# Landmark attention and a gated MLP on one core: the landmark values are folded into the gate and value weights

## The chip, the cores and the metric

The kernel runs on one core of a Trainium2 chip. Its time is the device time of one execution in microseconds (us). Five engines work side by side, each through its own list of instructions in order: TensorE (PE) multiplies matrices, VectorE (DVE), ScalarE (ACT) and GpSimd (POOL) work element by element, and SyncE (SP) issues the transfers (DMA) between the chip's main memory (HBM) and the on-chip memory (SBUF). PE writes its sums into eight PSUM banks, each 128 partitions by 512 fp32 values.

## The reference

The inputs are q, k and v (8 batches, 8 heads, 576 rows, 64 wide), three weight matrices in fp64 and a gain.

```python
q_lm = q.reshape(B, H, m, S // m, D).mean(axis=3)      # m = 32 landmarks
k_lm = k.reshape(B, H, m, S // m, D).mean(axis=3)
A, Bm, C = sm(q, k_lm), sm(q_lm, k_lm), sm(q_lm, k)    # sm: softmax of a.b^T / 8
Z = Bm^T / (|Bm|_1 |Bm|_inf)
for _ in range(6): Z = 2 * Z - Z @ Bm @ Z
attn = A @ Z @ C @ v
x = attn.transpose(0, 2, 1, 3).reshape(4608, 512)
xn = x / sqrt(mean(x * x) + 1e-6) * rms_g
out = (silu(xn @ w_gate) * (xn @ w_val)) @ w_out       # d_ff = 1536
```

For one batch and head, A is 576x32 and W = Z C v is 32x64. The rows of x for a batch are the eight products A W side by side, 8 x 64 = 512 wide.

## The kernel before, in words

Most products are split for accuracy: an operand is rounded to fp32r (`hi`), the rest is a second operand (`lo`), and a product is the three matmuls hi.hi, hi.lo, lo.hi. Rounding is an ACT copy, the rest a DVE or POOL subtraction.

**Attention.** Eight heads form two groups `g` of four. `stage1` sums q and k over blocks of 18 rows (`lmT`, L341), makes the scores `sC` and `sA` in PSUM, and the softmax of C on rows. Its `back` part does the softmax of A in transposed blocks `tA`, turns it into `AT`, splits that into `AS`, transposes E and makes `pCV` = C v. `newton` iterates with `PV`, which holds Z and Z C v together, and ends with `Whi` and `Wlo`. `second` makes x of a batch (`pO`, copied into `xr`), its mean square (`pss`, `pms`), the reciprocal root, and scales x by it and by the gain (L586). x goes to HBM (`x_dram`) and, split into `xhi` and `xlo` (L612, L614), into chunk tiles.

**MLP, direct part.** `d_ff` is 12 slices of 128. `mlp_chunk` takes 512 tokens through the first four slices: for gate and for value 12 matmuls of 512 columns over a contraction of 512, then silu on ACT (L269), product on DVE (L270), the split of the hidden slice (L273, L274), then output matmuls `pso` by groups of 128 tokens, whose partial sums go to HBM (`p_dram`). There are nine chunks. Seven are interleaved with the attention of later batches; the order is written by `Mixer`, which keeps a clock of assumed matmul times and lets attention parts in when their waits are due. All engines then run in the order so written.

**MLP, Strassen part.** After attention two passes take four slices each, through six units of 768 tokens. Gate and value together are multiplied by a 7-product scheme on halves (`product`, 384 columns, contraction 256, six matmuls each), with sums on DVE and splits of seven operands per unit from reloaded x (`prepare`, L825 and L826). Each pass loads partial sums, adds (L941) and stores. Weights arrive as fp64; `Weights` and `Fast` decode them on ACT and DVE (L725 to L733) tile by tile.

Of the kernel before, what the change touches and what calls it, by code (L numbers as in the profile page):

```python
# [79 lines left out]
def nystrom_moe_kernel(  # L80
# [18 lines left out]
    DFF = w_gate.shape[1] // 2  # L99
    M = 32  # L100
# [13 lines left out]
    mxs = ExitStack()  # L114
    mx_ = mxs.enter_context(tc.tile_pool(name="mx", bufs=2, reuse_waits="tile"))
# [12 lines left out]
    VZ = cst.tile([P, G, 3 * D], F32, name="VZ")  # L128
    nc.gpsimd.memset(VZ, 0.0)
# [15 lines left out]

    class Weights:


        def __init__(self, slots):
            self.slots = dict(slots)  # L150
            self.plan([(f, nm) for f, _ in slots for nm in "gv"] + [(f, "o") for f, _ in slots])
            self.done = {}

        def plan(self, order):
            self.order, self.queue, self.raws = list(order), list(order), {}

        def get(self, f, nm):
            while (f, nm) not in self.done:
                self.load_next()
            return self.done[f, nm]  # L160
# [17 lines left out]
        def load_next(self):  # L178
# [3 lines left out]
            slot = self.slots[f]  # L182
# [4 lines left out]
            wf = mp.tile(shp, F32, name="w32", tag="w32", bufs=WB)  # L187
            w = wf.bitcast(I32)
            nc.scalar.activation(wf, whead.bitcast(F32), AF.Abs)
            nc.vector.tensor_scalar_max(wf, wf, 2.0**-15)  # L190
# [685 lines left out]
    def unit(u, fs, xs, hs, src, last, after):  # L876
# [92 lines left out]
        for _ in nxt:  # L969
            pass  # L970
# [79 lines left out]
```

## Time and profile before

| | |
|---|---|
| timed runs (3) | median 1067.74 us, 1064.79 to 1068.96 |
| span of the profiled execution | 1067.6 us, mean granted PE clock 0.958 |
| PE, PEld (weight loads) busy | 1005.0 us (94%), 838.9 us (79%) |
| DVE, ACT, POOL busy | 738.9 us (69%), 485.2 us (45%), 90.0 us (8%) |
| transfers | 123.82 MB, mean 116 GB/s |
| first and second chunk's first hidden slice | 85.5 us, 160.1 us |

The profile gives the profiled execution's time as its span; it lies 0.1 us under the median of the timed runs, so nothing outside the span has to be added. A row of a group of instructions names line, engine, operation, output and inputs, shapes and count, then busy time, mean ns of one, idle time of the engine before them and what ended it. A row in order of time begins with start and length in us.

### The profile page before, as it was taken

To read this page: it belongs to the slowest core of one execution; us is meant where nothing else is said; L and a number is where in the kernel's file an instruction comes from. 1 tells how busy PE (TensorE), PEld (TensorE's weight loads), DVE (VectorE), ACT (ScalarE), POOL (GpSimd) and SP (SyncE) were. 2 spreads that over 40 slices of the span, in tenths; PEclk is the share of its full clock that TensorE was granted. 3 is DMA by queue.
4 is the path that set the end of the run, shared out by engine and by line. 5 is a ranking of instruction groups with operands and counts; after the bars stand their busy time and mean duration, and the time that the engine had idled before them with its cause. 6 is when DMAs were issued, how large, how long until landed. Compare 5 with 4: busy or idle time off the path is not lost.

```text
span 1067.6 us, 17593 instructions
## 1 busy us (share of the span) xinstructions
PE 1005.0 (94%) x6918; PEld 838.9 (79%) x6918; DVE 738.9 (69%) x1503; ACT 485.2 (45%) x988; POOL 90.0 (8%) x86
## 2 busy tenths in 40 slices
PE   5649989999999999999999999999999999999998
PEld 4326655676767677787989899998989989899997
DVE  7899959848565452787895665847897475675743
ACT  3536554446353533455644352433745344352431
POOL 2243221203020110100000000000000000000000
PEclk7669989999999999999999999999999999999999
DMA  9346443505130110543534505143250422505122
GB/s 336 118 141 204 145 148 96 190 23 196 64 111 34 53 64 21 182 131 97 180 114 151 170 8 178 34 144 130 88 177 20 160 87 91 177 1 177 50 69 79
DMA packets 62946, 123.82 MB, mean 116 GB/s; under 512 B 5520, under 2 KB 27024, under 8 KB 61840
## 3 DMA queue, kind: packets, MB, share of 16 engines
q1 hardware_dynamic: 62864, 122.71, 34.0%
q8 instruction: 54, 0.88, 0.4%
q14 instruction: 28, 0.23, 0.1%
HBM read 84.94 MB, written 37.75 MB: 115 GB/s over the span
## 4 chain that ended last, share of the span: by engine, by line
PE 74%; DVE 17%; DMA 3%; ACT 3%; issue 2%; POOL 1%; SPq 0%; ACTq 0%; DVEq 0%; POOLq 0%
PE pso L141 24%; PE px L141 18%; PE pz L141 9%; PE psg L141 6%; PE psv L141 5%; PE pw L141 4%; PE pO L141 2%; PE pn L141 2%; DVE xr L586 2%; DMA srawv<-in_moe_w_val_dram 1%; DVE lmT L341 1%; DVE h L274 1%; PE pCV L141 1%; DVE xlo L614 1%; DVE s L270 1%
## 5 line engine op out<-in xcount | busy, mean ns | idle before, releaser
L141 PE MATMUL pso<-whio,h 128*128 128x512 f32 x288 | 101.3, 421 | 6.1 <-DVE h L274 3.2
L141 PE MATMUL pso<-solo,h 128*128 128x512 f32 x432 | 100.4, 390 | 0.0
L825 ACT CAST x<-xf 128x768 fp32r<-128x768 f32 x84 | 68.0, 833 | 69.7 <-DVE xf L843 54.2
L141 PEld LDWEIGHTS pso<-solo,h 128*128 128x128 f32 x432 | 81.0, 188 | 16.3
L141 PE MATMUL pso<-sowhio,h 128*128 128x512 f32 x288 | 90.9, 390 | 0.0
L941 DVE TENSOR_TENSOR ob<-ob,pso 128x512 f32<-128x512 f32 x72 | 48.8, 684 | 49.1 <-PE pso L141 48.8
L826 DVE TENSOR_TENSOR x<-xf,x 128x768 fp32r<-128x768 f32 x84 | 79.1, 953 | 5.0 <-ACT x L825 5.0
L873 DVE TENSOR_TENSOR h<-c,h 128x384 fp32r<-128x384 f32 x96 | 53.2, 554 | 37.5 <-ACT h L872 37.5
L141 PE MATMUL psg<-xhi,whig 128*128 128x512 f32 x144 | 61.1, 424 | 16.5 <-ACT xhi L612 16.5
L141 PEld LDWEIGHTS pso<-whio,h 128*128 128x128 f32 x288 | 57.0, 200 | 22.7 <-DVE h L274 5.1
L894 ACT COPY c<-px 128x384 f32<-128x384 f32 x48 | 23.0, 480 | 109.3 <-PE px L141 109.3
L872 ACT CAST h<-c 128x384 fp32r<-128x384 f32 x96 | 49.5, 515 | 34.5 <-DVE c L883 28.2
L141 PE MATMUL psg<-xlo,whig 128*128 128x512 f32 x144 | 60.9, 423 | 2.8 <-DVE xlo L614 2.5
L141 PEld LDWEIGHTS pso<-sowhio,h 128*128 128x128 f32 x288 | 54.1, 188 | 11.0
L141 PE MATMUL pso<-wloo,h 128*128 128x512 f32 x144 | 60.5, 420 | 0.0
L141 PE MATMUL psg<-xhi,wlog 128*128 128x512 f32 x144 | 60.3, 419 | 0.0
L141 PE MATMUL px<-x,swfs1c 128*128 128x384 f32 x288 | 57.8, 334 | 1.3 <-ACT c L901 1.3
L141 PE MATMUL psv<-xhi,whiv 128*128 128x512 f32 x144 | 58.4, 406 | 0.0
L141 PE MATMUL psv<-xlo,whiv 128*128 128x512 f32 x144 | 58.3, 405 | 0.0
L141 PE MATMUL psv<-xhi,wlov 128*128 128x512 f32 x144 | 57.9, 402 | 0.0
L141 PE MATMUL px<-x,swfs2c 128*128 128x384 f32 x288 | 57.8, 335 | 0.0
L141 PE MATMUL px<-x,swfs0c 128*128 128x384 f32 x288 | 57.8, 335 | 0.0
(223 smaller groups left out, 2226.7 us busy)
## 6 DMA issues: line engine op xcount, KB each, us to landing
xd<-xr SPq DMA_DIRECT2D x8, 1152.0 KB, 5.0
pd<-ob SPq DMA_DIRECT2D x36, 256.0 KB, 2.2
xf<-xd SPq DMA_DIRECT2D x8, 1152.0 KB, 7.1
ob<-pd SPq DMA_DIRECT2D x36, 256.0 KB, 3.4
pe<-ob SPq DMA_DIRECT2D x36, 256.0 KB, 2.7
ob<-pe SPq DMA_DIRECT2D x36, 256.0 KB, 3.1
out_dram<-ob SPq DMA_DIRECT2D x36, 256.0 KB, 2.7
vt<-in_v_dram SPq DMA_DIRECT2D x16, 512.0 KB, 4.3
```

The costliest lines, as they stand in the source:

```text
L141: tc.keep_in_program_order(nc.tensor.matmul(*args, **kw))
L270: nc.vector.tensor_mul(s, s, banks[1])
L274: nc.vector.tensor_sub(h2, s, h1.bitcast(F32))
L341: nc.vector.tensor_reduce(lmT[:, z], qk[z].rearrange("p h (m c) -> p h m c", c=LM), axis=AX.X, op=ALU.add)
L586: last = nc.vector.scalar_tensor_tensor(xr[:, kk], xr[:, kk], gsb[:, kk : kk + 1], Rt, op0=ALU.mult, op1=ALU.mult)
L614: eng.tensor_sub(xlo[:, kk, off : off + n], xr[:, kk, pos : pos + n], xhi[:, kk, off : off + n].bitcast(F32),)
L825: nc.scalar.copy(t[:, 0], src)
L826: nc.vector.tensor_sub(t[:, 1], src, t[:, 0].bitcast(F32))
L872: nc.scalar.copy(hi, s)
L873: nc.vector.tensor_sub(lo, s, hi.bitcast(F32))
L894: nc.scalar.copy(c1, px)
L941: nc.vector.tensor_add(ob, ob, bank.pop(t))
```

## The change

x is never made for the MLP. Since x = A W by heads, `xn @ w` = (A/rms) @ (W gain w): `mix_weights` multiplies, for each batch and each pair of slices, the gate and value weights (fp32, 512 columns: gate and value of two slices) by the batch's landmark values `WT` (transposed, with the gain). The result (`pM`, split into `Mhi`, `Mlo`) has 8 x 32 = 256 rows. `second` still makes x once to get its mean square (`pO` is only squared), then scales `tA` by the reciprocal root, transposes, splits it into `an` and stores it to HBM for the second pass. `mlp` then multiplies `Mhi`/`Mlo` by `an`, 2 x 3 matmuls of 288 columns for each of gate and value and each half of a batch's 576 tokens. The Strassen code goes. There are two passes of six slices; the first, interleaved with attention, stores partial sums, the second reloads `an` and the partial sums and adds. A batch holds 4.5 groups of 128 tokens, so odd batches first copy the last 64 columns of each hidden slice on POOL (the `TAIL` copy). The maximum in the weights' decoding moves from DVE to POOL; gate and value weights are no longer split. The pool `pg` has four PSUM banks, before three; after attention nothing takes the other four.

```diff
--- before.py
+++ after.py
...
-            wf = mp.tile(shp, F32, name="w32", tag="w32", bufs=WB)
+            if nm == "o":
+                wf = mp.tile(shp, F32, name="w32", tag="w32", bufs=WB)
+            else:
+                pair = f // 2
+                if pair not in self.gv:
+                    self.gv[pair] = self.place("gv", pair), []
+                at = (f % 2 * 2 + "gv".index(nm)) * P
+                wf = self.gv[pair][0][:, :, at : at + P]
+                self.gv[pair][1].append(nm)
             w = wf.bitcast(I32)
             nc.scalar.activation(wf, whead.bitcast(F32), AF.Abs)
-            nc.vector.tensor_scalar_max(wf, wf, 2.0**-15)
+            nc.gpsimd.tensor_scalar_max(wf, wf, 2.0**-15)
...
-            hi = wp.tile(shp, F32R, name=f"whi{nm}{f}", tag=f"whi{nm}{slot}", bufs=1)
-            lo = wp.tile(shp, F32R, name=f"wlo{nm}{f}", tag=f"wlo{nm}{slot}", bufs=1)
-            nc.scalar.copy(hi, wf)
-            nc.gpsimd.tensor_sub(lo, wf, hi.bitcast(F32))
-            self.done[f, nm] = (hi, lo)
+            if nm == "o":
+                hi, lo = self.place("o", f)
+                nc.scalar.copy(hi, wf)
+                nc.gpsimd.tensor_sub(lo, wf, hi.bitcast(F32))
+                self.out[f] = hi, lo
...
-    def mlp_chunk(i, wts, fs, xhi, xlo, between=lambda: None):
-        nf = len(fs)
-        hh, hl = [], []
-        for fi, f in enumerate(fs):
...
+    def weight_order(f0):
+        fs = range(f0, f0 + NF1)
+        return [(f, nm) for f in fs for nm in "gv"] + [(f, "o") for f in fs]
...
+    def mix_weights(wts, b, pair):
+
+        wgv = wts.get("gv", pair)
+        ps = [pg.tile([P, 4 * P], F32, name="pM", tag="pg") for g in range(G)]
+        for h in range(4):
+            for g in range(G):
+                n = pos(g, h)
+                mm(
+                    ps[g][rows(n), :],
+                    WT[half(h), b, 2 * g + h // 2, rows(n % 2)],
+                    wgv[half(h), 2 * g + h // 2, :],
+                    start=True,
+                    stop=True,
+                )
+        hi = mp.tile([P, G, 4 * P], F32R, name="Mhi", tag="Mhi", bufs=2)
+        lo = mp.tile([P, G, 4 * P], F32R, name="Mlo", tag="Mlo", bufs=2)
+        for g in range(G):
+            nc.scalar.copy(hi[:, g], ps[g])
+            nc.vector.tensor_sub(lo[:, g], ps[g], hi[:, g].bitcast(F32))
+        mixed[b, pair] = hi, lo
+
+    hs = [wp.tile([P, 2, TAIL + S], F32R, name=f"h{f}", tag=f"h{f}") for f in range(NF1)]
+
+    def mlp(wts, b, f0, an, store, part, following):
+        pairs = [f0 // 2 + n for n in range(NPAIR)]
+        if (b, pairs[0]) not in mixed:
+            mix_weights(wts, b, pairs[0])
+            yield 1.1
+        for n, pair in enumerate(pairs):
+            if n + 1 < NPAIR and (b, pairs[n + 1]) not in mixed:
+                mix_weights(wts, b, pairs[n + 1])
+                yield 1.1
+            mhi, mlo = mixed.pop((b, pair))
+            for i in range(2):
+                s = mp.tile([P, S], F32, name="s", tag="s", bufs=2)
+                for e in range(2):
+                    cols = slice(e * HS, (e + 1) * HS)
+                    banks = []
+                    for z in range(2):
+                        ps = pg.tile([P, 512], F32, name=f"ps{'gv'[z]}", tag="pg")
+                        at = slice((2 * i + z) * P, (2 * i + z + 1) * P)
+                        for g in range(G):
+                            for w, a in ((mhi, 0), (mhi, 1), (mlo, 0)):
+                                mm(
+                                    ps[:, :HS],
+                                    w[:, g, at],
+                                    an[:, a, g, cols],
+                                    start=(g == 0 and w is mhi and a == 0),
+                                    stop=(g == G - 1 and w is mlo),
+                                )
+                                yield MMG
+                        banks.append(ps[:, :HS])
+                    nc.scalar.activation(s[:, cols], banks[0], AF.Silu)
+                    nc.vector.tensor_mul(s[:, cols], s[:, cols], banks[1])
+                h = hs[2 * n + i]
+                if b % 2:
+                    nc.gpsimd.tensor_copy(h[:, :, :TAIL], h[:, :, S : S + TAIL])
+                nc.scalar.copy(h[:, 0, TAIL:], s)
+                nc.vector.tensor_sub(h[:, 1, TAIL:], s, h[:, 0, TAIL:].bitcast(F32))
+        t0 = (b * S + P - 1) // P if b % 2 == 0 else b * S // P
+        t1 = (b + 1) * S // P
+        base = b * S - TAIL
+        groups = list(range(t0, t1))
+        obs = {t: part(t) for t in groups[:2]}
+        for at in range(0, len(groups), 2):
+            some = groups[at : at + 2]
+            bank = {t: pg.tile([P, DM], F32, name="pso", tag="pg") for t in some}
+            order = [(t, n) for t in some for n in range(NF1 - 1)] + [(t, NF1 - 1) for t in some]
+            for t, n in order:
+                sl = slice(t * P - base, (t + 1) * P - base)
+                hi, lo = wts.get("o", f0 + n)
+                mm(bank[t], hs[n][:, 0, sl], hi, start=(n == 0), stop=False)
+                yield MMO
+                mm(bank[t], hs[n][:, 0, sl], lo, start=False, stop=False)
+                yield MMO
+                mm(bank[t], hs[n][:, 1, sl], hi, start=False, stop=(n == NF1 - 1))
+                yield MMO
+                if n == NF1 - 1:
+                    store(t, bank[t], obs.pop(t))
+            for t in groups[at + 2 : at + 4]:
+                obs[t] = part(t)
+            if at == 0 and following():
+                mix_weights(wts, b + 1, pairs[0])
+                yield 1.1
...
-            Whi = sm.tile([P, 2, P], F32R, name="Whi", tag="Whi", bufs=1)
-            Wlo = sm.tile([P, 2, P], F32R, name="Wlo", tag="Wlo", bufs=1)
-            pW = pa.tile([P, 2, P], F32, name="pW", tag="pa")
...
+                    r = rows(rho(g, h))
+                    mm(pW[rows(pos(g, h)), g], Bs[r, g, :], VF[r, g, :], start=True, stop=True)
+            W = sm.tile([P, 2, 2, D], F32, name="W", tag="W", bufs=2)
+            nc.vector.tensor_copy(W, pW.unsqueeze(2).broadcast_to([P, 2, 2, D]))
+            nt["W"] = W
+            yield 0.4, WW
+            pT = pa.tile([P, NK, 2 * M], F32, name="pT", tag="pa")
+            for g in range(2):
+                tp(
+                    pT[:, 2 * g : 2 * g + 2].rearrange("p j n -> p (j n)"),
+                    W[:, g].rearrange("p a d -> p (a d)"),
+                    ident,
+                )
+            nc.vector.tensor_mul(WT[:, b], pT, gsb.unsqueeze(2).broadcast_to([P, NK, 2 * M]))
+            yield 0.3, WW
+            stage["wt"] = b
...
-            (Whi, Wlo), ATs = nt["W"], nt["AT"]
-            xr = ap.tile([P, NK, S], F32, name="xr", tag="xr", bufs=2)
...
+                po = [pa.tile([P, HS], F32, name="pO", tag="pa") for n in range(4)]
+                for h in range(4):
+                    for g in range(2):
+                        r = rows(pos(g, h))
+                        mm(po[2 * g + h // 2][half(h)], W[r, g, 0, :], ATs[g][r, cols], start=True, stop=True)
+                sq = ap.tile([P, NK, HS], F32, name="sq", tag="sq", bufs=2)
+                for n in range(4):
+                    nc.scalar.activation(sq[:, n], po[n], AF.Square)
+                sqs.append(sq)
+                yield 0.8, OWL
...
-            for kk in range(NK):
-                last = nc.vector.scalar_tensor_tensor(
-                    xr[:, kk], xr[:, kk], gsb[:, kk : kk + 1], Rt, op0=ALU.mult, op1=ALU.mult
-                )
-            nc.sync.dma_start(x_dram[b], xr)
...
+            an = mp.tile([P, 2, 2, S], F32R, name="an", tag="an", bufs=2)
+            for g in range(2):
+                eng = nc.gpsimd if g else nc.vector
+                eng.tensor_mul(tAs[g], tAs[g], r1.unsqueeze(2).broadcast_to([P, NB, M]))
+            for g in range(2):
+                af = ap.tile([P, S], F32, name="af", tag="af", bufs=1)
+                nc.vector.transpose(af, tAs[g].rearrange("p n m -> p (n m)"))
+                nc.scalar.copy(an[:, 0, g], af)
+                last = nc.vector.tensor_sub(an[:, 1, g], af, an[:, 0, g].bitcast(F32))
+            nc.sync.dma_start(a_dram[b], an.bitcast(F32).rearrange("p a g s -> p (a g s)"))
+            ans[b] = an
...
-    class Fast:
...
-    def product(ps, ws, xs, p, start):
...
-    def unit(u, fs, xs, hs, src, last, after):
...
+        def keep(t, ps, ob):
+            ob = mp.tile([P, DM], F32, name="ob", tag="ob", bufs=2)
+            nc.scalar.copy(ob, ps)
+            nc.sync.dma_start(p_dram[t], ob)
...
+    def load_an(b):
+        an = lp.tile([P, 2, 2, S], F32R, name="anl", tag="anl", bufs=2)
+        nc.sync.dma_start(an.bitcast(F32).rearrange("p a g s -> p (a g s)"), a_dram[b])
+        return an
...
+    def finish(t, ps, ob):
+        nc.vector.tensor_add(ob, ob, ps)
+        nc.sync.dma_start(out[t * P : (t + 1) * P, :], ob)
+
+    late = Weights(weight_order(NF1), place_late)
+    mix.add(late.stream(WAIT1 / 2))
+    mix.fill(mlp(early, B - 1, 0, ans.pop(B - 1), keep, lambda t: None, lambda: False))
+    nxt = load_an(0)
+    for b in range(B):
+        an, nxt = nxt, load_an(b + 1) if b + 1 < B else None
+        mix.fill(mlp(late, b, NF1, an, finish, load_part, lambda b=b: b + 1 < B))
```

How the order of instructions moves. First, PE where the second half of the program begins. Before, one slice of a Strassen unit: `px`, `pz`, `pw` are the products' banks, `x` the seven split operands, `swfs0c` the weights.

```order
L141 MATMUL px<-x_5426,swfs0c_5092 128x384 x6
L141 MATMUL pz<-x_5430,swfs0c_5096 128x384 x6
L141 MATMUL px<-x_5434,swfs0c_5097 128x384 x6
L141 MATMUL pw<-x_5437,swfs0c_5093 128x384 x6
L141 MATMUL pz<-x_5440,swfs0c_5094 128x384 x6
L141 MATMUL px<-x_5444,swfs0c_5098 128x384 x6
L141 MATMUL px<-x_5426,swfs1c_5263 128x384 x6
L141 MATMUL pz<-x_5430,swfs1c_5267 128x384 x6
```

These rows stand no more in the changed program.

Now, where the second pass begins, with two mixes and the first gate/value sections (`anl` is the reloaded attention weights, `lgv` the late weights):

```order
L104 MATMUL pM<-lgv_5927,WT 32x512 x8
L104 MATMUL pM<-lgv_6050,WT 32x512 x8
L104 MATMUL psg<-anl,Mhi 128x288 x2
L104 MATMUL psg<-anl,Mlo 128x288
L104 MATMUL psg<-anl,Mhi 128x288 x2
L104 MATMUL psg<-anl,Mlo 128x288
L104 MATMUL psv<-anl,Mhi 128x288 x2
L104 MATMUL psv<-anl,Mlo 128x288
L104 MATMUL psv<-anl,Mhi 128x288 x2
L104 MATMUL psv<-anl,Mlo 128x288
```

Products of 384 columns in runs of six are replaced by mixes of eight matmuls and sections of six with 288 columns.

Second, DVE in the front of the program, around the first hidden slices. Before, around the first slice's product (L270) and split (L274) of the first chunk; `w_1041` is a weight tile in decoding, `lmT` a landmark sum:

```order
L190 TENSOR_SCALAR w_1041<-w_1041 128x512
L405 TENSOR_REDUCE mA<-tA 128x18
L191 TENSOR_SCALAR w_1041<-w_1041 128x512
L270 TENSOR_TENSOR s<-s,psv 128x512
L489 TENSOR_TENSOR PV<-p_992,nden 128x2x32
L388 TENSOR_TENSOR ss<-ss 128x1
L194 SCALAR_TENSOR_TENSOR w_1041<-wrawv_1039,w_1041 128x512
L389 TENSOR_SCALAR ss<-ss 128x2
L341 TENSOR_REDUCE lmT<-qk_984 128x64
L390 RECIPROCAL rs<-ss 128x2
L274 TENSOR_TENSOR h_1005<-s,h_1005 128x512
```

Of this, the maximum (L190) leaves DVE and the chunk's product and split become those of half and whole batches.

Now, around the second hidden slice of the first batch (L288 product, L293 split):

```order
L288 TENSOR_TENSOR s<-s,psv 128x288
L170 TENSOR_SCALAR wgv_799<-wgv_799 128x4x128
L414 TENSOR_REDUCE mA<-tA 128x18
L293 TENSOR_TENSOR h_130<-s,h_130 128x576
L173 SCALAR_TENSOR_TENSOR wgv_799<-wrawv_1001,wgv_799 128x4x128
L170 TENSOR_SCALAR w_1030<-w_1030 128x512
L176 SCALAR_TENSOR_TENSOR wgv_799<-wrawv_1001,wgv_799 128x4x128
L173 SCALAR_TENSOR_TENSOR w_1030<-wrawo_1028,w_1030 128x512
L418 TENSOR_REDUCE sumA<-tA 128x18
L176 SCALAR_TENSOR_TENSOR w_1030<-wrawo_1028,w_1030 128x512
L419 TENSOR_SCALAR sumA<-sumA 128x18
L347 TENSOR_REDUCE lmT<-qk_989 128x64
```

More weight tiles of the MLP and landmark sums of later batches (L347; the last row is of the fourth batch) stand among the first batch's hidden slices; the maximum of a weight tile is no longer a row here (it was L190).

More of the change, by code (lines that the diff above doesn't have):

```diff
@@ L144, in tp, with rho, pos, rows @@
         tc.keep_in_program_order(nc.tensor.transpose(*args))
-    class Weights:
[L149 to L158, printed above, removed]
+    def rho(g, h):
+        return h if g else h ^ 1
+    def pos(g, h):
+        return rho(g, h) ^ 1
+    def rows(n):
+        return slice(n * M, (n + 1) * M)
+    def half(h):
+        return slice(h % 2 * D, (h % 2 + 1) * D)
+    class Weights:
+        def __init__(self, order, place):
+            self.order, self.queue = list(order), list(order)
+            self.place = place
+            self.raws, self.gv, self.out = {}, {}, {}
+        def get(self, kind, f):
+            done = self.gv if kind == "gv" else self.out
+            while f not in done or (kind == "gv" and len(done[f][1]) < 4):
                 self.load_next()
-            return self.done[f, nm]
+            return done[f][0] if kind == "gv" else done[f]
         def fetch(self, tag=None):
@@ L528, in new_state @@
                 "AT": [None, None],
+                "tA": [None, None],
             }
-        def first(b):
-            new_state(b)
-            for g in range(2):
-                yield from stage1(b, g)
         state = {}
@@ L630, in nystrom_moe_kernel @@
+        early = Weights(weight_order(0), place_early)
+        for g in range(2):
+            load_qk(0, g)
         for g in range(2):
@@ L668, in nystrom_moe_kernel @@
         load_qk(1, 0)
-        for u in range(F1):
-            early.fetch(f"h{u}")
+        early.fetch()
         load_v(1, 0)
-        for u in range(F1, F2):
-            early.fetch(f"h{u}" if u < NFA else None)
+        early.fetch()
         mix.add(seconds(), True)
         mix.add(newtons(), True)
-        mix.add(early.stream(WAIT0, NCV))
+        mix.add(early.stream(WAIT0, 4))
         mix.drain(lambda: stage["newton"] >= 0)
@@ L972, in nystrom_moe_kernel @@
-    xs_next, load_next, lxs = {}, [], []
-    mix.add(fast.stream(plan_a[:NFA], WAIT1))
-    for i in range(B - 1, NCH):
-        if i == NCH - 1:
-            first_x = load_x(0)
-        def between(i=i):
-            if i < NCH - 1:
-                return
-            mxs.close()
-            lxs.append(ctx.enter_context(tc.tile_pool(name="lx", bufs=1, reuse_waits="tile")))
-            for _ in prepare(first_x, xs_next):
-                pass
-            mix.add(fast.stream(plan_a[NFA:], WAIT1))
-        mix.fill(mlp_chunk(i, early, fs, *chunks.pop(i), between))
```

574 lines of the change are left out of this document (86 added, 488 removed).

## The prediction

> **What bounds the kernel now.** I read the chain of waits first, then the busy time by stretch, then the groups of instructions, then the order of time around single matmuls.
>
> ```profile
> PE 74%; DVE 17%; DMA 3%; ACT 3%; issue 2%; POOL 1%; SPq 0%; ACTq 0%; DVEq 0%; POOLq 0%
> ...
> 0.00:85.50 85.50, 47.96 (x629) 31.24 (x637) 75.02 (x183) 37.63 (x89) 26.82 (x29) 0.68 0.59 202
> 85.50:160.00 74.50, 68.35 (x749) 43.67 (x733) 60.26 (x146) 43.27 (x93) 19.92 (x15) 0.91 0.47 160
> 160.00:437.00 277.00, 265.55 (x2359) 190.37 (x2358) 174.11 (x438) 126.91 (x275) 43.26 (x42) 0.98 0.25 86
> ...
> 515.00:790.00 275.00, 273.68 (x1441) 256.02 (x1440) 196.16 (x335) 126.55 (x241) 0.00 (x0) 1.00 0.36 121
> 790.00:1068.00 278.00, 273.91 (x1443) 256.14 (x1441) 169.19 (x277) 109.47 (x210) 0.00 (x0) 1.00 0.29 97
> ```
>
> The chain is TensorE (PE) for 74% and VectorE (DVE) for 17%. The stretches (us, then PE, weight loads, DVE, ACT, POOL busy, granted clock, DMA) say where: to 160 us DVE is busy 135 of 160 and PE runs at a clock of 0.68 to 0.91; after 515 us PE never rests. The bounds at 85.5 and 160 are the first hidden slices of the first and second chunk:
>
> ```profile
> 85.49 0.66 DVE L274 TENSOR_TENSOR h<-s,h 128x512 fp32r<-128x512 f32 x1
> 160.09 0.68 DVE L274 TENSOR_TENSOR h<-s,h 128x512 fp32r<-128x512 f32 x1
> ```
>
> **The price of a matmul.** Busy spans of matmuls overlap, so the price is the step from start to start.
>
> ```profile
> 800.74 1.20 PE L141 MATMUL pw<-x,swfs0c 128*128 128x384 f32 x6
> 801.78 1.20 PE L141 MATMUL pz<-x,swfs0c 128*128 128x384 f32 x6
> ...
> 826.82 0.61 PE L141 MATMUL pso<-sowhio,h 128*128 128x512 f32 x2
> 827.50 0.61 PE L141 MATMUL pso<-sowhio,h 128*128 128x512 f32 x2
> ```
>
> Six matmuls of 384 columns take 1.04 us: 173 ns each. Three of 512 take 0.68: 227 ns. The line through both is 0.418 ns a column and 13 ns fixed, which gives 133.5 ns for 288 columns. The check: a Strassen unit has 168 of the first and 72 of the second, 45.5 us; six make 273, and the last stretch holds 273.9 busy. A floor by the weight loads would spoil the line, so I looked for shorter steps:
>
> ```profile
> 259.20 0.30 PE L141 MATMUL pO<-AS,Whi 64*128 64x288 f32 x2
> 259.34 0.30 PE L141 MATMUL pO<-AS,Wlo 64*128 64x288 f32 x2
> ...
> 260.79 0.60 PE L144 MATMUL sE<-ident,E 128*128 128x128 f32 x4
> 261.23 0.27 PE L144 MATMUL sF<-ident,E 128*64 128x128 f32 x1
> ```
>
> Pairs with 288 columns follow each other at 0.14, and transposes with full 128x128 weights at 0.44 / 4 = 0.11. A load therefore hides behind less than 133 ns. Ends for the unseen case (288 columns, 128 rows): 0.11 and 0.173; I take 0.1335, nearest to the pO row.
>
> **What goes and what comes on PE.** Gate/value before: 864 matmuls of 512 and 2016 of 384, 196.6 + 349.4 = 546 us. Now 16 batch passes of 6 slices, 144 matmuls of 288 columns each: 2304 x 0.1335 = 308. Output: 1296 of 512 both times, 295 us. New are 48 weight mixes of 8 fp32 matmuls (16 records, 512 columns, weights 64x32). Their nearest rows:
>
> ```profile
> 278.17 0.39 PE L141 MATMUL psv<-xhi,wlov 128*128 128x512 f32 x1
> 278.49 1.18 PE L141 MATMUL pss<-sq,ones 128*32 128x288 f32 x16
> 279.60 0.50 PE L141 MATMUL psv<-xhi,whiv 128*128 128x512 f32 x1
> ...
> 289.18 0.43 PE L141 MATMUL sC<-qk,lmT 64*32 64x288 f32 x1
> 289.44 0.40 PE L141 MATMUL sC<-qk,lmT 64*32 64x288 f32 x1
> ```
>
> The score matmuls have the same 64x32 weights: eight records start together and the next eight 0.25 us later, 0.85 ns a column, twice the price above. At 512 columns that is 0.43; two rounds, 0.87, and 0.1 at each change of shape (the gap before pss: 278.17 to 278.49, less one step of 0.227): 1.05 us, 50 us for 48. Ends: 0.87 without changes, 16 x 0.227 = 3.6 if nothing ran together.
>
> Each mix leaves two of the four banks to ACT (about 0.6 us a bank) and DVE (0.68), some 2 us in sequence; the order puts a pair of slices (6.4 us) ahead of the first reader, but the banks are wanted again after 1.6 us: about 0.2 us of wait a mix, counted below.
>
> Attention on PE I estimate at 13.5 us a batch before (along the timeline of one batch, in steps like the 1.11 of pss) and 12.6 now: pO loses a third of its matmuls, pT comes. So PE as a whole loses 546 - 308 - 50 + 7 = 195 us. The span of the profiled execution, 1067.6, stands 0.1 under the median of the runs; with all stalls kept, 873 would be left.
>
> **The front, which DVE sets.** By the order in which the changed program issues, DVE does more before the second batch's first hidden slice: 22 landmark sums instead of 20, 18 early weight tiles instead of 12, the lower halves of five mixes, and the first batch's hidden slices are six instead of four. DVE is in order, so I add its rows up to that mark.
>
> ```profile
> L341 DVE TENSOR_REDUCE lmT<-qk 128x64 f32<-128x1152 f32 x28 | 37.4, 1340 | 3.1 <-DMA qk<-in_q_dram 3.1
> L941 DVE TENSOR_TENSOR ob<-ob,pso 128x512 f32<-128x512 f32 x72 | 48.8, 684 | 49.1 <-PE pso L141 48.8 <-DMA ob<-pe 0.2
> L904 DVE TENSOR_TENSOR c<-c,pw 128x384 f32<-128x384 f32 x48 | 26.5, 551 | 42.1 <-PE pw L141 42.0
> L394 DVE STREAM_TRANSPOSE tA<-sA 128x288 f32<-128x288 f32 x32 | 14.5, 467 | 0.2
> L375 DVE TENSOR_REDUCE mx<-sC 128x1 f32<-128x288 f32 x32 | 14.1, 440 | 11.0 <-PE sA L141 10.9
> L497 DVE SCALAR_TENSOR_TENSOR PV<-PV,pn 128x192 f32<-128x192 f32 x40 | 13.9, 348 | 26.7 <-PE pn L141 26.5
> L418 DVE TENSOR_TENSOR AS<-AT,AS 128x576 fp32r<-128x576 f32 x16 | 12.7, 793 | 2.2 <-ACT AS L417 2.2
> L415 DVE STREAM_TRANSPOSE AT<-tA 128x576 f32<-128x576 f32 x16 | 12.3, 771 | 4.6 <-POOL tA L413 4.6
> L405 DVE TENSOR_REDUCE mA<-tA 128x18 f32<-128x576 f32 x16 | 11.9, 744 | 0.0
> L726 DVE TENSOR_SCALAR sw<-sw 128x512 f32<-128x512 f32 x24 | 10.1, 422 | 11.7 <-ACT sw L725 11.3
> L730 DVE SCALAR_TENSOR_TENSOR sw<-srawg,sw 128x512 int32<-128x512 int32 x8 | 5.5, 686 | 0.1
> L412 DVE RECIPROCAL rA<-sumA 128x18 f32<-128x18 f32 x16 | 4.0, 249 | 0.1
> ```
>
> 22 landmark sums x 1.34 = 29.5; 18 tiles x (0.42 + 2 x 0.69) = 32.4; 18 score transposes 8.4 and 18 maxima 7.9; 18 reductions x 0.74 = 13.4; 18 Newton steps 6.3; 12 transposes x 0.77 = 9.3; 10 differences of 576 x 0.79 = 7.9; 14 products of 288 columns at 0.45 (the line through L904 and L941) 6.3; 10 mix halves x 0.68 = 6.8; two scalings of tA, between 0.79 and 1.34, near the first, at 0.95; 171 short ones x 0.25 = 43. Sum 173 us. Before, DVE idled 24.7 us up to the same kind of mark (160 - 75.0 - 60.3); I keep that: the mark falls at 198, 38 later than before, with more done.
>
> **The rest.** After the mark PE still has 2136 gate/value matmuls (285), 1224 output matmuls (279), 43 mixes (45) and about four batches of attention, 52: 661 us. In the old stretch from 160 to 437 PE's work was some 191 of chunks and 50 of attention, so 36 of 277 us were lost. The new one has five batches (252 us of PE) against 169 of DVE, and shorter banks: a pair fills in 1.6 us, before 5.4. I take the same 14%: 35.
>
> ```profile
> srawo<-in_moe_w_out_dram SPq DMA_DIRECT2D x8, 512.0 KB, 3.8
> wrawg<-in_moe_w_gate_dram SPq DMA_DIRECT2D x4, 512.0 KB, 6.1
> xf<-xd SPq DMA_DIRECT2D x8, 1152.0 KB, 7.1
> ```
>
> (Last column: us from issue to landing.) Late weights: 18 tiles come through two buffers, each held for the landing and some 3.5 us of decoding on ACT, POOL and DVE: (3.8 + 3.5) / 2 = 3.7 us a tile, 66 us, or 86 with the slower landing. The last is read some 69 us after the stream begins (batch seven's 43, a batch's gate/value part, six output slices). I take 5, and 3 for bank waits. The end, from the last output matmul through sum and store, is 4 as before. The attention weights' store and reload (1.2 MB a batch) stand where x did on SP's queue, and one of the two rounds of partial sums is gone: nothing, with DMA at 0.29 in the last stretch; the first reload is asked for a batch (43 us) ahead, and without that cover it costs its 7.1. **Sum: 198 + 661 + 35 + 8 + 4 = 906; I say 905 us.**
>
> **Rivals.** (a) *POOL and DVE exclude each other in the front*, 949 us, 7%. The change gives POOL the weights' maximum (18 before the mark, unseen, near 1 us) and a scaling beside the two tA steps.
>
> ```profile
> L413 POOL TENSOR_TENSOR tA<-tA,rA 128x576 f32<-128x576 f32 x16 | 20.1, 1256 | 54.7 <-DVE rA L412 24.3 <-DVE r L575 8.1 <-DVE PV L489 8.1
> ...
> L190 DVE TENSOR_SCALAR w<-w 128x512 f32<-128x512 f32 x12 | 6.8, 566 | 0.5 <-ACT w L189 0.5
> ```
>
> POOL's work there is about 44 us; all of it added to DVE gives 949. For it: L190, the same step as L726, takes 566 instead of 422 ns while POOL works. Against it: to 160 us DVE and POOL are busy 135 + 47 = 182, so they did run together. The Trainium skill, SBUF — State Buffer, Who interferes with whom, has this as an exclusive lock, for DVE instructions with two SBUF inputs or in a two-port mode; the 144 ns of L190 fit a part of that, the overlap says not the whole.
>
> (b) *The front is no longer than before*, 872 us, 12%: PE needs only some 72 us between the two marks, and DVE may idle less than it did. Against it stand 173 us of rows.
>
> (c) *Eviction sets the gate/value sections*, 982 us, 6%. Four banks serve them; a silu (about 0.45; 0.52 is the row of 384 columns) and a product (0.45) must end within the 1.6 us of the next pair. If the silu is no longer covered, and waits behind table loads and hidden-slice steps, 0.4 at each of 192 pairs puts 77 us on top.
>
> ```profile
> L905 ACT ACTIVATE c<-c 128x384 f32<-128x384 f32 x48 | 25.2, 524 | 35.8 <-DVE c L904 35.7
> ```
>
> The Trainium skill, TensorEngine Tiling (Array Packing), Performance Considerations, says that packing speeds up matmuls but not the copy out of PSUM, which may become the bottleneck: by that rule the mixes would add to this case; no row of this kernel shows a mix.
>
> (d) *Slower: the weight load stays exposed in front of each short matmul*, 3%. Place: the 2304 gate/value matmuls; price 188 ns of load ahead of 120 ns of columns: 0.308 x 2304 - 308 is 402 us more, 1307. It decides from 0.204 us a matmul. Against it: 384 columns at 0.173 already hide their loads.
>
> ```profile
> L141 PEld LDWEIGHTS px<-x,swfs2c 128*128 128x128 f32 x288 | 50.8, 188 | 0.5
> ```
>
> The Trainium skill, TensorE: Matmul & The Clock Gate, Part 3: Packing small matmuls — row/col tiling, says that loads overlap running matmuls only where the row groups differ; by that (d) would hold, and the 0.173 rows contradict it.
>
> **Numbers.** The forecast has 72%, by itself 870 to 945: the mark 185 to 215, stalls 15 to 60, a matmul 0.130 to 0.140 (15 us). With (b) and most of (a) the range is 862 to 965. A measurement here tells 0.5% from nothing. Only (d) and accidents end above 1073: faster 0.96, same 0.01, slower 0.03.
>
> **What would show it.** Gate/value matmuls at 133 ns; mixes near 1.05 us, eight records at once; the second batch's first hidden slice near 198 us with DVE busy over 85% until then; the second pass as eight periods alternating 38.7 and 42.8 us, 325 in all; PE busy from 250 us on. Wrong would be a step above 0.15 us, second-pass periods above 43 us, or first-pass batches above 65 us after the mark.

## The result, and the profile after

The changed kernel takes 925.74 us (median of four runs, 924.3 to 927.44) against 1066.26 us beside it: a ratio of 0.868, 95% interval 0.865 to 0.870. The forecast was 905 us in a range of 862 to 965. The profiled execution spans 922.5 us. One execution in what follows, the profiled one of the run e_dve_late, took 1312 us at a granted clock of 0.553 and is left out.

The changed kernel's busy time by stretch (columns as before: us, PE, weight loads, DVE, ACT, POOL, granted clock, DMA share). The bounds are the second batch's first hidden slice, the seventh batch's, and the first of the second pass:

```profile
0.00:189.40 189.40, 130.18 (x1671) 86.94 (x1671) 154.26 (x367) 83.79 (x181) 63.66 (x58) 0.77 0.53 174
189.40:483.50 294.10, 277.03 (x2834) 208.62 (x2834) 165.82 (x424) 133.21 (x273) 28.36 (x32) 0.98 0.21 74
483.50:590.60 107.10, 93.60 (x578) 75.73 (x572) 64.95 (x121) 44.39 (x88) 39.23 (x31) 0.90 0.44 144
590.60:922.50 331.90, 328.26 (x2119) 273.46 (x2117) 127.38 (x222) 88.61 (x185) 7.11 (x24) 1.00 0.23 76
```

PE is full only in the last stretch. The third is the odd one: two batches with hardly any attention left, which in the second pass take 83.8 us, take 107.1 here, at a clock of 0.90 and with POOL busy for 39 us.

The steps of single matmuls in the second pass, in order of time (start, length):

```profile
645.51 0.43 PE L104 MATMUL psv<-anl,Mhi 128*128 128x288 f32 x2
645.77 0.30 PE L104 MATMUL psv<-anl,Mlo 128*128 128x288 f32 x1
645.91 0.43 PE L104 MATMUL psv<-anl,Mhi 128*128 128x288 f32 x2
...
653.06 0.63 PE L104 MATMUL pso<-lhio,h 128*128 128x512 f32 x2
653.53 0.40 PE L104 MATMUL pso<-lloo,h 128*128 128x512 f32 x1
653.76 0.63 PE L104 MATMUL pso<-lhio,h 128*128 128x512 f32 x2
...
654.46 0.39 PE L104 MATMUL pso<-lhio,h 128*128 128x512 f32 x1
654.78 1.09 PE L104 MATMUL pM<-lgv,WT 64*32 64x512 f32 x16
655.80 0.50 PE L104 MATMUL pso<-lhio,h 128*128 128x512 f32 x1
```

Three matmuls of 288 columns take 0.40 us, 133 ns each, as forecast. Three output matmuls take 0.70, not 0.68: 233 ns. From the last output matmul ahead of a mix to the first behind it are 1.34 us, less one step 1.11: the mix, forecast at 1.05.

What the decoding of weight tiles looks like now: the groups of POOL's maximum, then what DVE waited for (total us, times, longest):

```profile
L169 POOL TENSOR_SCALAR lgv<-lgv 128x512 f32<-128x512 f32 x12 | 18.9, 1575 | 34.7 <-ACT lgv L168 34.7
L169 POOL TENSOR_SCALAR wgv<-wgv 128x512 f32<-128x512 f32 x12 | 18.9, 1575 | 24.8 <-ACT wgv L168 24.8
L169 POOL TENSOR_SCALAR w<-w 128x512 f32<-128x512 f32 x12 | 18.4, 1531 | 7.8 <-ACT w L168 7.8
```

```profile
DVE lgv L170 <- POOL lgv L169: 20.1, 12, 4.9
...
DVE w L170 <- POOL w L169: 16.6, 10, 3.5
...
DVE wgv L170 <- POOL wgv L169: 8.1, 5, 2.9
```

The step that took DVE 0.57 us takes POOL 1.55, and DVE stands 45 us waiting for it.

### The profile page after: what moved, and what is told of

Read it like the earlier page. It is cut to its first block, busy times and chain, and to the rows that moved or that the text cites. A ratio compares the mean times of both kernels' runs of the same rounds, so it can differ in the third digit from the quotient of the medians.

```text
span 922.5 us, 17461 instructions
## 1 busy us (share of the span) xinstructions
PE 829.1 (90%) x7190; PEld 644.8 (70%) x7190; DVE 512.4 (56%) x1131; ACT 350.0 (38%) x726; POOL 138.4 (15%) x145
## 4 chain that ended last, share of the span: by engine, by line
PE 70%; DVE 11%; ACT 6%; DMA 5%; POOL 4%; issue 3%; SPq 0%; DVEq 0%; ACTq 0%; POOLq 0%
PE pso L104 30%; PE psg L104 15%; PE psv L104 14%; PE pM L104 4%; DMA wrawv<-in_moe_w_val_dram 2%; PE pn L104 2%; DMA wrawg<-in_moe_w_gate_dram 2%; POOL w L169 2%; ACT L287 1%; DVE lmT L347 1%; ACT sq L555 1%; POOL lgv L169 1%; PE pss L104 1%; PE pCV L104 1%; DVE Mlo L253 1%
## 5 line engine op out<-in xcount | busy, mean ns | idle before, releaser
L104 PE MATMUL pso<-lhio,h 128*128 128x512 f32 x432 | 138.8, 396 | 0.0
L288 DVE TENSOR_TENSOR s<-s,psv 128x288 f32<-128x288 f32 x192 | 85.3, 447 | 68.9 <-PE psv L104 54.0
L287 ACT ACTIVATE s<-psg 128x288 f32<-128x288 f32 x192 | 77.8, 411 | 87.3 <-PE psg L104 87.1
L104 PE MATMUL psg<-an,Mhi 128*128 128x288 f32 x384 | 90.4, 318 | 15.5 <-ACT an L588 8.5
L252 ACT CAST Mhi<-pM 128x512 fp32r<-128x512 f32 x96 | 51.5, 589 | 135.2 <-PE pM L104 135.2
L293 DVE TENSOR_TENSOR h<-s,h 128x576 fp32r<-128x576 f32 x96 | 74.3, 774 | 46.2 <-ACT h L292 46.2
L104 PEld LDWEIGHTS pso<-lhio,h 128*128 128x128 f32 x432 | 81.0, 187 | 24.9 <-DVE obl L689 5.9
L104 PE MATMUL psv<-an,Mhi 128*128 128x288 f32 x384 | 85.4, 309 | 3.0 <-DVE s L288 1.6
L104 PE MATMUL psg<-anl,Mhi 128*128 128x288 f32 x384 | 83.1, 305 | 4.0 <-DVE Mlo L253 4.0
L104 PE MATMUL pso<-lloo,h 128*128 128x512 f32 x216 | 85.2, 395 | 0.0
L689 DVE TENSOR_TENSOR obl<-obl,pso 128x512 f32<-128x512 f32 x36 | 24.7, 687 | 107.8 <-PE pso L104 107.7
L104 PE MATMUL psv<-anl,Mhi 128*128 128x288 f32 x384 | 80.6, 299 | 0.0
```

What stands on the lines that cost most here:

```text
L104: tc.keep_in_program_order(nc.tensor.matmul(*args, **kw))
L252: nc.scalar.copy(hi[:, g], ps[g])
L287: nc.scalar.activation(s[:, cols], banks[0], AF.Silu)
L288: nc.vector.tensor_mul(s[:, cols], s[:, cols], banks[1])
L293: nc.vector.tensor_sub(h[:, 1, TAIL:], s, h[:, 0, TAIL:].bitcast(F32))
L689: nc.vector.tensor_add(ob, ob, ps)
```

## The experiments

Each is the changed kernel with the edit shown. The mark at which the second batch's first hidden slice comes varies: in five kernels with the same front (the changed one, and the runs e_buf3, e_out_early, e_align and e_no_late) it lies at 186.8 to 195.2 us.

### The maximum back on DVE, late tiles only, or all

```diff
-            nc.gpsimd.tensor_scalar_max(wf, wf, 2.0**-15)
+            (nc.vector if self.late else nc.gpsimd).tensor_scalar_max(wf, wf, 2.0**-15)   # e_dve_late
+            nc.vector.tensor_scalar_max(wf, wf, 2.0**-15)                                 # e_dve_all
```

> The maximum of the late weight tiles goes back to DVE; the early ones stay on POOL. Theory L (the 107 us from the seventh batch's first hidden slice at 483.5 to the second pass's first at 590.6 hold some 82 us of matmul steps and are stretched by the 18 late tiles, which pass at 5.1 us each, 1.5 of them the maximum on POOL): a tile at about 4.2 us, the second pass's first hidden slice near 578, the whole near 913 us. Rival (the landing of 3.6 to 5.5 us in two buffers sets the tile, whatever the engines do): within 3 us of 925.

> The maximum of all weight tiles on DVE, as in the kernel before. Beside the run that moves only the late ones, this shows the front. Theory F (DVE's rows set the front): 18 maxima of 0.5 us come on top of DVE's rows, second batch's first hidden slice 4 to 9 us later than 189.4, the whole 4 to 9 us above the run with only the late ones moved. Rival (the front waits for POOL: DVE stood 12 us behind POOL's maximum): that slice at 180 to 187, the whole 3 to 9 us under that run.

Measured: 913.96 us with the late tiles moved (913 to 921), 906.89 with all (904 to 911). Of the second, the maximum on DVE and the stretches (same bounds):

```profile
L169 DVE TENSOR_SCALAR w<-w 128x512 f32<-128x512 f32 x12 | 6.7, 562 | 5.7 <-ACT w L168 5.7
...
L169 DVE TENSOR_SCALAR wgv<-wgv 128x512 f32<-128x512 f32 x12 | 5.0, 416 | 3.2 <-ACT wgv L168 3.2
```

```profile
0.00:180.00 180.00, 127.25 (x1671) 83.02 (x1671) 156.24 (x385) 83.81 (x181) 35.96 (x40) 0.80 0.55 184
180.00:473.90 293.90, 277.17 (x2834) 208.79 (x2834) 165.87 (x425) 133.21 (x273) 28.39 (x32) 0.98 0.22 74
473.90:572.10 98.20, 88.02 (x574) 73.14 (x572) 73.60 (x139) 44.24 (x88) 12.07 (x13) 0.97 0.48 157
572.10:904.10 332.00, 328.38 (x2118) 273.52 (x2117) 127.24 (x222) 88.60 (x185) 7.13 (x24) 1.00 0.22 76
```

The move to POOL costs 18.9 us of time, 11.8 of it by the late tiles. By the stretches it is 8.9 us in the third and 9.4 in the front, where with the maximum on DVE that engine has 18 instructions more and is done earlier. The front's part is more than scatter: three kernels with the maximum on DVE (this one, e_best and e_best3) have the mark at 178.4 to 180.0 us, the five with it on POOL at 186.8 or later. The second and fourth stretch stay within 0.2. Theory F, that DVE's rows alone set the front, falls: they fill 154 to 156 us of either front, and what differs is the idle time between them, 35 against 24 us; 12 of the 35 end with POOL's maximum.

### Issuing the maximum a tile ahead

```diff
+            self.ready = self.head()     # next tile: abs on ACT, maximum on POOL
             ... DVE's three steps of this tile
```

> The maximum stays on POOL for all tiles, but the sign removal on ACT and the maximum on POOL of a tile are issued one tile ahead of DVE's three steps, so DVE no longer stands in front of a maximum that has just begun. Theory W (18.8 us of the changed program are the wait of DVE, in its order, for POOL's 1.55 us): DVE's 53 us of waits for the maximum mostly go, second batch's first hidden slice near 180, the whole 903 to 911 us. Rival X (POOL and DVE exclude each other at the port, or POOL's busy time itself counts): the waits go but rows on DVE and POOL lengthen, the whole 918 to 927 us.

Measured: 925.14 us. This told nothing apart: DVE's waits didn't go (20.2 us for the late `lgv` tiles, 20.1 in the changed kernel). The edit changed the order of issue and not the time at which a maximum could start, because the raw tile isn't there earlier. The order of time of this run shows one round of a raw buffer: DVE's last step with it, the load that follows at once, ACT's first step, the last step again, the next load.

```profile
513.25 0.68 DVE L185 SCALAR_TENSOR_TENSOR lgv<-wrawg,lgv 128x512 int32<-128x512 int32 x1
...
514.01 0.38 SPq L148 DMA_DIRECT2D wrawg<-in_moe_w_gate_dram  x1
...
518.03 0.66 ACT L168 ACTIVATE lgv<-wrawg 128x512 f32<-128x512 f32 x1 [6.73 <-DMA wrawg<-in_moe_w_gate_dram]
...
521.48 0.69 DVE L185 SCALAR_TENSOR_TENSOR lgv<-wrawg,lgv 128x512 int32<-128x512 int32 x1
...
522.20 0.38 SPq L148 DMA_DIRECT2D wrawg<-in_moe_w_gate_dram  x1
```

Of the 16 late tiles that come into a used buffer, 13 start on ACT within 0.1 us of their landing, in this run and in the changed kernel.

### POOL busy on a tile nobody waits for

```diff
-            nc.gpsimd.tensor_scalar_max(wf, wf, 2.0**-15)
+            nc.vector.tensor_scalar_max(wf, wf, 2.0**-15)
+            for _ in range(4):
+                nc.gpsimd.tensor_scalar_max(dum, sel.rearrange("p a b -> p (a b)"), 2.0**-15)
```

> The maximum of all tiles on DVE, and at the place of each POOL works as long as its maximum did, on a small tile of its own that nobody waits for (four steps of 128 columns with their operand in SBUF). It tells why POOL's maximum cost 18.8 us. Theory W (those who wait for it: DVE's next step, and through it the buffers and TensorE): as with the maximum on DVE, 903 to 911 us. Theory X (POOL's work as such takes DVE's access to SBUF away, or keeps POOL from the attention's scalings): 916 to 928 us; half of it: between.

Measured: 958.09 us, outside both. The steps, which wait for nothing, all ran between 9.8 and 108 us and kept POOL from the attention's scalings; the first hidden slice came at 127 instead of 77 us. So it doesn't measure the wait. It does show DVE beside a POOL that is busy for 80.6 of the first 100 us. The group of POOL, and of DVE from 9.8 to 108 us a decoding step with two operands in SBUF; below it the same step in the run with the maximum on DVE and POOL mostly idle:

```profile
L172 POOL TENSOR_SCALAR dum<-sel 128x128 bf16<-128x128 f32 x144 | 82.6, 574 | 19.9 <-DVE sel L91 8.5
...
L176 DVE SCALAR_TENSOR_TENSOR wgv<-wrawg,wgv 128x512 int32<-128x512 int32 x4 | 2.9, 716 | 0.0
```

```profile
L173 DVE SCALAR_TENSOR_TENSOR wgv<-wrawg,wgv 128x512 int32<-128x512 int32 x6 | 4.0, 673 | 0.0
```

Beside POOL's one-operand steps, which fill most of that time, DVE loses a few hundredths of a us (0.716 against 0.673; the other such steps 0.68 to 0.71 against 0.68 to 0.70), and beside POOL's maximum in the changed kernel at most 0.3 in a single row. Other rows of the changed kernel are a whole us late, and its order of time (POOL, then DVE) shows which POOL work stood beside them:

```profile
129.81 1.29 POOL L182 TENSOR_TENSOR wloo<-w,whio 128x512 fp32r<-128x512 f32 x1
132.41 1.48 POOL L422 TENSOR_TENSOR tA<-tA,rA 128x576 f32<-128x576 f32 x1 [1.31 <-DVE rA L421]
```

```profile
129.87 1.51 DVE L170 TENSOR_SCALAR w<-w 128x512 int32<-128x512 int32 x1 [0.43 <-POOL w L169]
...
132.80 1.70 DVE L293 TENSOR_TENSOR h<-s,h 128x576 fp32r<-128x576 f32 x1
```

Work on POOL with two operands in SBUF: the DVE row that starts inside it ends 0.3 to 0.6 us after it, 0.95 to 1.1 us late. Not all DVE rows are late beside such work: in the changed kernel reductions, transposes, reciprocals and rows with an operand in PSUM that start inside these POOL steps keep their length within 0.06 us. The Trainium skill (SBUF — State Buffer, Who interferes with whom) has an exclusive lock between a DVE instruction with two SBUF inputs, or in a two-port mode, and a POOL instruction that reads SBUF. The rows beside POOL's two-operand steps show such a lock; those beside its one-operand steps don't. In the front it is small: the lengthened groups of the changed kernel add up to some 4 us (L293 1.9, L399 1.1, L173 1.1).

### A third buffer for late tiles

```diff
-            raw = mp.tile(shp + [2], I32, tag="wraw", bufs=2)
+            raw = (lp if third else mp).tile(shp + [2], I32, tag="wraw3" if third else "wraw", bufs=1 if third else 2)
```

(`third`: every third tile of the late ones.)

> A third buffer for the raw late tiles, all else as changed. Theory L with landing and decoding in series in two buffers: the landing goes behind the decoding, a tile near 4.2 us, the whole 910 to 917 us. Rival (the chain ACT, POOL, DVE of decoding sets the tile in the order of issue): within 3 us of 925.

Measured: 920.28 us, 5.5 less, between the two expectations. The late tiles finish one per 3.9 us instead of 4.7 (last DVE step of the first to that of the eighteenth: 66.2 and 79.6 us, over 17), but the third stretch loses only 5.6: 101.5 us. The landing is part of it, and not all. By the order of time of the changed kernel a raw buffer is taken 4.0 us by the landing and then 5.4 by the decoding, up to DVE's last step (means of the 16 late tiles that come into a used buffer): 9.4 us in two buffers are the 4.7 a tile. With the maximum on DVE it is 4.1 and 4.2, and a tile per 4.1 us.

### No late weights at all

```diff
-    late = Weights(weight_order(NF1), place_late)
-    mix.add(late.stream(WAIT1 / 2))
+    late = Late()          # gives the tiles of the first six slices again
```

> The second pass uses the first pass's weights again; the 18 late tiles are neither loaded nor decoded (the output is another). It prices all that the late weights cost. Theory L (the 107 us between the seventh batch's and the second pass's first hidden slice hold 82 to 86 us of matmul steps, the rest is the late tiles): 83 to 87 us there, and 4 us less behind it for the output steps at 0.227, the whole 898 to 904 us. Rival (those 107 us are stalls of the last attention steps and of the banks): over 912 us.

Measured: 897.9 us. Third and fourth stretch:

```profile
482.50:567.70 85.20, 84.60 (x571) 71.23 (x572) 32.26 (x67) 30.80 (x64) 3.44 (x7) 1.00 0.22 83
567.70:896.00 328.30, 324.64 (x2119) 273.73 (x2117) 127.15 (x222) 88.64 (x185) 7.05 (x24) 1.00 0.23 77
```

The late weights cost 107.1 - 85.2 = 21.9 us, where the prediction had 5. By the rows 12.9 of them are idle time of PE (13.5 against 0.6) and 9.0 a longer busy time for the same matmuls (93.6 against 84.6), at a clock of 0.90 instead of 1.00. How they cost it stands in the changed kernel's order of time at the start of the second pass (DVE, ACT, then PE):

```profile
578.00 0.43 DVE L170 TENSOR_SCALAR w<-w 128x512 int32<-128x512 int32 x1 [3.48 <-POOL w L169]
```

```profile
579.92 0.62 ACT L181 CAST lhio<-w 128x512 fp32r<-128x512 f32 x1 [3.60 <-DVE w L176]
580.44 0.66 ACT L168 ACTIVATE w<-wrawo 128x512 f32<-128x512 f32 x1
581.00 2.03 ACT L252 CAST Mhi<-pM 128x512 fp32r<-128x512 f32 x4
```

```profile
576.37 1.96 PE L104 MATMUL pM<-lgv,WT 64*32 64x512 f32 x14 [1.53 <-ACT ob L658]
582.35 0.85 PE L104 MATMUL psg<-anl,Mhi 128*128 128x288 f32 x2 [4.03 <-DVE Mlo L253]
...
585.58 0.68 PE L104 MATMUL psv<-anl,Mhi 128*128 128x288 f32 x2
586.06 0.44 PE L104 MATMUL psv<-anl,Mlo 128*128 128x288 f32 x1
586.30 0.68 PE L104 MATMUL psg<-anl,Mhi 128*128 128x288 f32 x2
```

The mix is done at 578, but its copy (L252) stands on ACT behind two steps of the decoding, and the first of them waits 3.6 us for DVE, which waited 3.5 for POOL's maximum. So PE waits 4 us for the copy of a mix. Of PE's 13.5 idle us in this stretch 5.7 end with such a copy, and 5.4 with a copy out of an output bank (`ob`, L658), which stands in the same queue on ACT; none ends with a weight tile that comes too late to be multiplied. The clock has dropped by then as well (stretches of 10 us; it was 1.00 before):

```profile
565.00:575.00 10.00, 7.31 (x36) 3.46 (x34) 5.51 (x7) 3.90 (x7) 5.61 (x4) 0.85 0.44 135
575.00:585.00 10.00, 4.07 (x21) 2.00 (x22) 4.13 (x8) 4.43 (x9) 5.44 (x4) 0.50 0.32 103
585.00:595.00 10.00, 10.00 (x71) 9.00 (x69) 5.42 (x10) 4.66 (x10) 1.88 (x3) 0.80 0.00 1
```

While PE has these gaps the granted clock goes to 0.50 (without the late weights, with 0.6 us of gaps, it stays at 1.00), and the gate/value matmuls behind them begin at half speed (585.58 to 586.30: 0.24 us each).

### The start address of the second pass's tiles

In the program all tiles of the second pass start 32 bytes behind a multiple of 64 bytes in a partition of SBUF, those of the first at one.

```diff
-                hi, lo = wts.get("o", f0 + n)
+                wts.get("o", f0 + n); hi, lo = early.get("o", n)     # e_out_early
```

```diff
+    pad = lp.tile([P, 8], F32, name="pad", tag="pad")                 # e_align
+    nc.gpsimd.memset(pad, 0.0)
```

> The second pass multiplies with the output weights of the first six slices again (it leaves out the late output weights, which are still loaded and decoded; the output is another). The output matmuls of the second pass step by 0.233 us, those of the first by 0.2275. If it is the place of the weight tiles: 0.2275 in the second pass, about 4 us less. If it is something else of that pass (the added partial sums, the lack of attention): 0.233 stays and the time within 2 us of 925.

> 32 bytes are added behind the second pass's tiles, so that each of them starts at a multiple of 64 bytes in SBUF and not 32 behind one; nothing else changes. If the start address makes the output matmuls of the second pass step by 0.233 us: they step by 0.227 as in the first pass, a pair of second-pass periods takes 82.9 instead of 83.8 us, the whole 921 to 922.5 us. If it is another property of the place: 0.233 stays, 924 to 927 us.

Measured: 922.9 and 923.87 us. Output matmuls of the run with 32 bytes more, in order of time:

```profile
651.62 0.62 PE L104 MATMUL pso<-lhio,h 128*128 128x512 f32 x2
652.07 0.39 PE L104 MATMUL pso<-lloo,h 128*128 128x512 f32 x1
652.30 0.62 PE L104 MATMUL pso<-lhio,h 128*128 128x512 f32 x2
```

0.68 for three, in both runs; so it is the start address of the weight tiles, shown by the second run, in which nothing else was changed. The fourth stretch takes 327.6 us against 331.9, with 0.7 of the 4.3 us in the matmuls of 288 columns, whose moving operand `anl` has moved too. The time of that run doesn't show it, since its front took 195.2 us, within the scatter named above.

### Fewer mixes; no table loads

```diff
         wgv = wts.get("gv", pair)
+        if b:                                  # e_nomix: products of batch 0 for all
+            mixed[b, pair] = kept[1 if pair % NPAIR == 1 else 2]
+            return
```

```diff
-                    nc.scalar.activation(s[:, cols], banks[0], AF.Silu)
+                    nc.scalar.activation(s[:, cols], banks[0], AF.Exp)      # e_exp
```

> Leaves out 42 of the 48 mixes: all batches of a pass use the products of batch 0 (the output is another). If a mix costs its TensorE time alone (1.11 us and 0.1 of waits): 21 go from the second pass, a pair of periods 83.8 - 7.2 = 76.6 us, and 42 in all, the whole 872 to 880 us. If the copies out of the banks count as well (ACT 0.59 and DVE 0.68 us for each of two banks): another 20 to 50 us, 825 to 860 us. If the stalls of the first pass take up what is freed: 890 to 900 us.

> The hidden slices use an exponential in place of the silu (the output is another), so that ACT needs no change of table between attention and hidden slices: 33 table loads of 1.28 us go. Theory T (about ten of them lie on the chain in the first pass, where some 33 us are stalls): 910 to 919 us. Rival (ACT, 56% idle or more there, hides them): 923 to 927 us.

Measured: 864.63 and 918.82 us. The fourth stretch without 21 of its mixes:

```profile
556.30:860.20 303.90, 300.03 (x1769) 268.92 (x1768) 101.03 (x180) 67.16 (x143) 8.87 (x25) 1.00 0.24 83
```

28.0 us for 21 mixes, 1.33 each; over all 42 it is 61.1 us, 1.45 each, between the first two expectations. Beyond the 1.11 us on PE that is 0.2 to 0.3 us a mix, so the copies (ACT 0.59 and DVE 0.68 us for each of two banks) are for the most part hidden. The table loads cost 6.9 us for 33, 5.7 of it in the second stretch (288.4 against 294.1; it takes 291.0 to 294.4 in the runs that leave it unchanged): ACT hides most of them, a sixth of their 42 us shows.

### The version that is faster than both

```diff
  the maximum on DVE for all tiles, the third buffer, the 32 bytes                 # e_best
+ the lower half of late output weights on DVE too                                 # e_best3
```

> The maximum of all tiles on DVE, a third buffer for late raw tiles, and tiles of the second pass that start at multiples of 64 bytes. If the three effects (18.8, 5.5 and about 4 us) add up but for what the first two share (both shorten the late tiles): 898 to 902 us, against 906.9 with the maximum alone; if the third buffer is worth nothing once the maximum is short: 902 to 904 us.

> As the run before, with the late output weights' lower half computed by DVE too (0.7 instead of 1.28 us). If the chain ACT, DVE, ACT, POOL of a late output tile still sets the start of the second pass: 1 to 4 us under that run; if the landing does: the same within 1.5 us.

Measured: 894.16 us (ratio to the kernel before 0.838, interval 0.835 to 0.841) and 894.09 us. Stretches of the first:

```profile
0.00:178.40 178.40, 125.89 (x1671) 82.20 (x1671) 155.87 (x385) 83.85 (x181) 35.92 (x40) 0.81 0.56 185
178.40:472.20 293.80, 277.16 (x2834) 208.84 (x2834) 165.74 (x424) 133.12 (x273) 28.34 (x32) 0.98 0.21 74
472.20:562.90 90.70, 86.30 (x575) 71.34 (x571) 73.88 (x138) 44.60 (x88) 12.02 (x14) 1.00 0.52 170
562.90:890.50 327.60, 324.01 (x2119) 272.92 (x2117) 127.07 (x222) 88.56 (x186) 7.04 (x24) 1.00 0.23 77
```

That is under both expected ranges, and some 3 us faster than the three effects together (925.7 - 18.9 - 5.5 - 4.3 = 897), which lies at the edge of its interval (891 to 897). In the third stretch the maximum and the buffer gain 16.4 us together against 8.9 + 5.6 alone, and PE keeps its clock at 1.00 there (0.90 in the changed kernel). The late tiles still cost 90.7 - 85.2 = 5.5 us, near the 5 of the prediction. With the lower halves on DVE too there is no difference in time; in the profiled execution the third stretch is 2.5 us shorter and the front 1.4 longer, so an effect of a us or two stays open.

## Why the prediction was right, and where it was not

Against the profiled execution's 922.5 us the sum of 906 was 16.5 short (20 by the medians): the front came 8.6 us early, the five batches behind it took 294.1 us instead of 252 + 35, and the rest 439.0 instead of 906 - 198 - 287 = 421. That 905 is within 2.3% of 925.7 is in part luck: without the 8.6 us of the front the sum would have been 25 short.

- **Matmuls of 288 columns: right.** 133 ns, from a line through 384 and 512 columns. It carries the gain: 2304 of them for 2880 longer ones, some 308 us for 546. Rival (d) falls with it.
- **Mixes: right in kind, small in size.** 1.05 us and 0.2 of wait each were forecast, not all of it in the sum; 1.11 on PE and 1.33 to 1.45 in all were measured. By the Trainium skill (TensorEngine Tiling (Array Packing), Performance Considerations) the copies out of PSUM may become the bottleneck where packing speeds up the matmuls. Here they did not: 0.2 to 0.3 us of some 2 us of copies show for each mix. PE waited for copies only where decoding stood in front of them. Rival (c) had a PE that waits at each pair; in the fourth stretch PE is busy for 328.3 of 331.9 us.
- **Output matmuls, 295 us "both times": wrong by 4 us.** The second pass's tiles have another start address, and 648 matmuls step by 0.233 instead of 0.227 us.
- **The front: two errors that nearly cancel.** The durations of DVE's rows up to the mark add up to 179 us (forecast 173), but they overlap at their ends: 154 us busy. The idle time of 24.7 was taken from busy time and added to a sum of durations, which doesn't fit; in the old front too 158 us of rows were 135 busy. Against that, the idle time grew to 35 us, 12 of it behind POOL's maximum.
- **"Late weights: I take 5": the step that failed.** They cost 21.9. The step had a tile at (3.8 + 3.5) / 2 = 3.7 us; measured were (4.0 + 5.4) / 2 = 4.7, so the decoding was the mis-sized term: the maximum takes 1.55 us on POOL and not near 1, and the steps wait for each other over ACT, POOL and DVE. And the step asked only whether the last tile is ready when it is read. No tile was late in that way; the decoding held up, in the in-order queue of ACT, the copies of the mixes and of the output banks, on which PE waits, and with PE's gaps the clock fell. With the maximum on DVE and a third buffer they cost 5.5.
- **Stalls of 35 in the five batches:** about 42 were there; table loads are 5.7 of them.
- **Rival (a)** had the right culprit and the wrong mechanism. The maximum on POOL cost 18.9 us; exclusion at SBUF is seen in single rows beside POOL steps with two operands, some 4 us of the front. DVE's busy time in the front isn't longer with the maximum on POOL (154 against 156 us), only its idle time is, and a late raw buffer is freed 1.2 us sooner after its landing without it. That these waits are the cause is read from the rows of both runs; neither run that was to separate waits from exclusion did so. Rival (b), a front no longer than 160 us, didn't happen: even the earliest mark stands at 178.
- **The marks:** the second pass ran in periods of 39.8 and 44.0 us, 335 in all, above the 43 that was to count as wrong: output steps (4 us over eight periods) and the mixes, at 1.33 instead of 1.05 us, make up the 9 us and a little more. The batch right behind the mark took 67.7 us, above the 65 that was to count as wrong; the next four took 47 to 64. DVE was busy for 81% of the front, not 85.

## What to carry to other kernels

A small step handed to an idle engine isn't free if the busy engine next needs its result: here 0.5 us less on DVE became 1.55 us in a chain through in-order queues, 19 us in all. Sum an engine's work by busy time of a stretch, not by adding durations of rows, when idle time is then added from the same stretch. Price a stream that feeds a stage by the whole chain of one buffer (landing, each engine, hand-overs), and look what else stands in the queues that it uses.

## What the runs showed of the hardware

- A 512-column matmul whose moving operand starts 32 bytes behind a multiple of 64 steps at 0.233 us, and at 0.227 when it starts at one.
- Matmuls of 288 columns with 128x128 weights step at 133 ns in the second pass; their weight loads of 191 ns stay hidden.
- POOL's maximum with a scalar over 128x512 floats takes 1.48 to 2.0 us, DVE's 0.42 where nothing disturbs it.
- An arithmetic or bit-wise DVE row with all operands in SBUF that starts during a two-operand POOL step ends after it (0.75 becomes 1.70 us), while reductions, transposes, reciprocals and rows with an operand in PSUM keep their length within 0.06 us; beside one-operand POOL steps of 0.57 us each, two-operand DVE rows take 0.68 to 0.72 us, against 0.67 to 0.70 beside an idle POOL.
- With waits of 2.5, 1.5 and 4.0 us on PE within 13 us the granted clock was 0.85, 0.50 and 0.80 in three successive stretches of 10 us, and matmuls of 288 columns right behind the waits stepped at 0.24 us.
